# A fused attention, MLP and expert mixture: the last period of the MLP in another order, operand sums on VectorE, and loads of attention at other places

## The chip, the cores and the metric

One core of one Trainium2 chip runs the whole network in one launch. The metric is the device time of that core in microseconds, a median over runs.

## The reference

Three stages follow one another; each one's output is the next one's x.

```python
def _attn_ref(q, k, v, centroids):           # B=2, H=8, S=768, D=64, 16 clusters
    q_assign = np.argmax(np.einsum('bhsd,hcd->bhsc', q_n, c_n), axis=-1)   # likewise k_assign
    mask = q_assign[:, :, :, None] == k_assign[:, :, None, :]
    scores = np.where(mask, scale * np.matmul(q, k.transpose(0, 1, 3, 2)), -1000000000.0)
    attn = np.exp(scores - np.max(scores, axis=-1, keepdims=True))
    return np.matmul(attn / (attn.sum(-1, keepdims=True) + 1e-09), v)

def _moe_ref(x, w_gate, w_val, w_out):       # x 1536 x 512, d_ff 1536
    return (1.0 / (1.0 + np.exp(-(x @ w_gate)))) * (x @ w_val) @ w_out

def _moe2_ref(x, domain_probs, w1, w2):      # 4 experts, hidden 1024
    p = domain_probs / (domain_probs.sum(-1, keepdims=True) + 1e-09)
    for e in range(E):
        out += p[:, e:e + 1] * (np.maximum(x @ w1[e], 0.0) @ w2[e])
```

## The kernel before

**Numbers.** Every fp32 operand of a matmul is split into a high part, made by ScalarE, and a low part, the difference, made by VectorE or GpSimd. A product is three matmuls: high by high, high by low, low by high. Large products also go through seven block products in place of eight; for that, sums of operand blocks are formed first. In the profile a name that ends in h is a high part, in l a low part.

**Attention** takes eight pairs of heads with twelve items each, about 31 us to a pair. An item makes the scores of 128 queries, the exponentials, their transposes and, two items later, the product with V. The work of the next pair is hung beside the items by the table SLOT (line 35): an entry names an item, counted from the first one of the pair, and a place in it. `load_q` and `load_k` fetch Q and K as nq and nk. `q0` to `k1` transpose them and write the parts hiq, loq, hik, lok (lines 257 to 270). `rows0` and `rows1` (line 387) copy these parts by DMA to the operands L and R of the two heads, six DMAs for each. For each head the product with V leaves PSUM as U (line 472), which two DMAs carry to A and W. `spread` sends the row sums out to DRAM as rd and fetches them back, repeated over 64 partitions, as rb (lines 498 and 501); `xadd` and `xscale` then make the MLP's input. SyncE issues every DMA of the kernel, in program order, and waits there when one is not ready. The table SOON sets where the first raw weights of the MLP are loaded and converted.

**MLP.** `moe1` (line 847) runs six periods p over 256 hidden columns each, for two batches b of 768 tokens. TensorE's stages come in the order gate(p, 0), outp(p-1, 1), value(p, 0), gate(p, 1), outp(p, 0), value(p, 1). `gate` and `value` call `seven` (line 776): products 1, 6, 7, 5, 2, 4, 3 of six matmuls each with 384 columns, and between them VectorE combinations (lines 806 to 828) and pieces of side work, one list entry after each product. `outp` makes eight blocks, two halves n by four d, of six matmuls each, and adds each to acc. With `soon` it first sends the matmuls of the first outer block f = 0 to four banks of PSUM, and then those of f = 1. The raw weights are 64-bit words: a conversion is two ScalarE operations (658, 660), three on VectorE (665 to 667) and one on GpSimd (672). After it come four sums of blocks (702), the highs (710) and the lows w1l (711) of a unit in four groups, vs0 to vs3, where vs2 holds product 7 and vs3 product 4. An outer block has woh and wol (768, 769). `normalise` (167) scales the expert weights with four small VectorE operations.

**Mixture.** `operands` (1003) makes four operand sums (1019) from acc and the splits of seven operands Y (1015, 1016). `moe2` (1059) runs 32 pairs: `hidden` with `seven`, and `outp` with 36 matmuls of 512 columns.

Of the kernel before, what the change touches and what calls it, by code (L numbers as in the profile page):

```python
# [28 lines left out]
def r2(ap):  # L29
# [6 lines left out]
    "load_q": (-25, 0), "load_k": (-24, 2), "load_v": (-5, 2), "sq_q": (-19, 0), "sq_k": (-19, 0),  # L36
# [30 lines left out]
    "load01": (20, 2), "abs01": (25, 2), "bits01": (27, 36, 37), "low01": (27, 2), "round01": (38, 2),  # L67
    "load00": (32, 2), "abs00": (37, 2), "bits00": (39, 48, 49), "low00": (39, 2), "round00": (50, 2),
    "loado": (56, 2), "abso": (60, 2), "bitso": (61, 62, 63), "lowo": (61, 2), "roundo": (64, 2),
# [10 lines left out]
class Net:  # L80
# [85 lines left out]
    def normalise(self):  # L166
        nc, c = self.nc, self.cpool
        s = c.tile([128, B * NT], F32, name="pns")
        v = self.pn.rearrange("p b t e -> p (b t) e")
        nc.vector.tensor_reduce(s, v, axis=AX.X, op=ALU.add)  # L170
        nc.vector.tensor_scalar(s, s, 1e-9, None, op0=ALU.add)
        nc.vector.reciprocal(s, s)
        nc.vector.tensor_tensor(v, v, s.unsqueeze(2).to_broadcast([128, B * NT, E]), op=ALU.mult)
# [308 lines left out]
    def finish(self, n):  # L482
# [9 lines left out]
        def spread():  # L492
# [4 lines left out]
            d = self.dr.tile([2 * NT, 128], F32, name="rd", tag="rd", bufs=2)  # L497
            nc.sync.dma_start(out=d, in_=rT)
# [13 lines left out]
        return [("recip", recip), ("spread", spread), ("xadd", xadd), ("xscale", xscale)]  # L512
# [29 lines left out]
    def attention(self):  # L542
# [100 lines left out]
        spread, xadd, xscale = [go for at in sorted(work) for go in work[at]]  # L643
        spread()
        for _, g in pvs:
            list(g)
# [200 lines left out]
    def moe1(self, xadd, xscale):  # L847
# [35 lines left out]
        def outp(p, b, work=(), soon=False):  # L883
# [13 lines left out]
            def evict(ps, d, n):  # L897
                a = acc[:, d, b * S + n * HB:b * S + n * HB + HB]
                if p == 0:
                    nc.scalar.activation(a, ps, AF.Copy)  # L900
                else:
                    nc.vector.tensor_tensor(a, a, ps, op=ALU.add)  # L902
                if work:
                    for go in work.pop(0):
                        go()

            for n in range(2):
                c = slice(n * HB, n * HB + HB)
                if soon:
                    banks = [bank() for _ in range(4)]  # L910
                    for some in ((0, 1), (2,)) if n == 0 and (p == 0 or b == 1) else (range(3),):
# [25 lines left out]
        def total(u):  # L937
            return [lambda: u["sums"](Q)]
# [18 lines left out]
        value(0, 1, [load(U[1][1])] + [[go] for go in U[1][0]["split"]] + [[self.normalise]])  # L957
        for p in range(1, NP):
# [3 lines left out]
            if p + 1 < NP:  # L962
                g = U[p + 1][0]
                for go in load(g):
                    go()
            else:
                self.load_in2(0)
                self.load_in2(1)
            c = conv(o0)
            outp(p - 1, 1, [[vs[0]], [vs[1]], [vs[2]] + c[0], [vs[3]] + c[1], c[2], c[3], c[4]])  # L970
# [3 lines left out]
            if p + 1 < NP:  # L974
                c, d, split = conv(g, 0), conv(g, 1), g["split"]
                gate(p, 1, [e[0], e[1], e[2], e[3] + e[4], [o1["split"]] + c[0], c[1] + c[2], c[3] + c[4]])
                outers[2 * p + 2]["load"]()
                outp(p, 0, [d[0], d[1], d[2], d[3] + d[4], total(g), [split[0]], [], [split[1]]], soon=True)
                value(p, 1, [load(U[p + 1][1]), [split[2]], [split[3]]])
        gate(NP - 1, 1, [e[0], e[1], e[2], e[3] + e[4], [o1["split"]]])  # L980
        self.load_out2(0)
        out, cin = self.conv_out2(0), self.conv_in2(0)
        outp(NP - 1, 0, [[lambda: cin[0](Q)], [], [], [cin[1]], [cin[2]], [cin[3]], [cin[4]], []])
        Y = {o: (room(self.xp, "h%d" % o), room(self.xp, "l%d" % o)) for o in (0, 3, 4)}
        Y[5] = room(self.nat0, "nk"), room(self.nat0, "nq")
        Y[6] = room(self.xp, "tA"), room(self.xp, "tB")
# [4 lines left out]
        cin = self.conv_in2(1)  # L991
        value(NP - 1, 1, [[ys[0]], [lambda: ysplit(0, V), ys[1]], [ys[2]], [], [], [], [ys[3], lambda: ysplit(4, V)]])
        outp(NP - 1, 1, [[out[0], out[1], lambda: self.load_out2(1), lambda: ysplit(5, V), lambda: cin[0](Q)], [],
                         [lambda: ysplit(3, V)], [cin[1]], [lambda: ysplit(1, V)], [lambda: ysplit(6, Q)],
                         [cin[2]], [cin[3], cin[4]]], soon=True)
        self.last_split = lambda: ysplit(2, V)
# [9 lines left out]
    def operands(self, b, room):  # L1006
# [11 lines left out]
        add = nc.gpsimd if b == 0 else nc.vector  # L1018
        sums = [lambda o=o, x=x, z=z: add.tensor_tensor(o, x, z, op=ALU.subtract)
# [37 lines left out]
    def moe2(self):  # L1057
# [5 lines left out]
        def hidden(i, work):  # L1063
# [10 lines left out]
            if i == 0:  # L1074
                work = [[self.last_split]] + [[], []] + work
            self.seven(self.win2.pop(i)["w"], self.Y, [t[:, i % 2] for t in temps], split, [[], []][:2 - (i == 0)] + work[:2] + [[]] + work[2:])
# [38 lines left out]
        for i in range(LAST):  # L1115
            if i + 2 < LAST:
                self.load_in2(i + 2)
            hidden(i, (self.conv_out2(i + 1) if i + 1 < LAST else []) + late)
# [10 lines left out]
            else:  # L1129

                gap = [lambda: None] * (3 if i in (1, PER + 1) else 0)
# [91 lines left out]
```

## Time and profile before

| | |
|---|---|
| median of three runs | 1078.47 us (1076.16 to 1079.19) |
| the profiled execution | 1079.04 us, its span 1077.0 us |
| TensorE matmul busy (PE) | 1037.7 us, 96% |
| VectorE / ScalarE / GpSimd busy (DVE, ACT, POOL) | 822.0 / 547.3 / 640.0 us |
| mean granted clock of TensorE | 0.992 |

Attention lies at about 31 to 284 us of the span, the MLP at 284 to 573, the mixture behind it. PE means matmuls, PEld weight loads, SP SyncE. A row of waits names the waiting engine and line, what ended the wait, then the total, the number of times and the longest. A row of windows gives for a stretch its length, and the busy time and instructions of each engine, then the granted clock, the share of the DMA engines and their rate. A row of the timeline gives the start, the duration (the sum, where rows are merged) and the instruction; in brackets is the engine's idle time before it and what ended that. A row of groups ends with busy time, mean ns of one, and idle time.

### The profile page before, as it was taken

The page shows a single profiled execution, that of the slowest core. Times are in us where ns is not written, and L with a number is a line of the kernel's source. Part 1 is how long each engine was busy: PE and PEld are TensorE (multiplying, and loading weights), DVE is VectorE, ACT ScalarE, POOL GpSimd, SP SyncE. Part 2 cuts the span into 40 slices and gives each one's busy share as a digit, 9 for nine tenths or more (in the row PEclk, how much of TensorE's full clock was granted, in tenths as well). Part 3 has the DMA queues.
Part 4 walks back from the last instruction along what each step waited for, and adds up shares of the span by engine and source line. Part 5 has one row for each costly group of instructions (what it writes and reads, how often), then busy time and mean ns, then how long its engine had stood idle before and what let it go on. Part 6 is the DMA issues. An engine that isn't in the chain of part 4 may idle for free. (4 is left out here: it accounts for less than half of the span.)

```text
span 1077.0 us, 16228 instructions
## 1 busy us (share of the span) xinstructions
PE 1037.7 (96%) x5813; PEld 962.8 (89%) x5813; DVE 822.0 (76%) x1404; ACT 547.3 (51%) x1155; POOL 640.0 (59%) x572
## 2 busy tenths in 40 slices
PE   6999989899989999999998999999999999999998
PEld 5899989898889999999997889989998999899887
DVE  6998989799886776877765877677668867776765
ACT  4888989789665444444443433333334433333320
POOL 7566777767876677676786644444445644444430
PEclk8999999999999999999999999999999999999999
DMA  8678767654212222212111222122122312221201
GB/s 177 139 165 189 180 150 174 139 134 135 65 40 60 60 78 79 64 54 79 59 40 59 79 79 61 58 79 79 50 69 99 118 41 77 79 78 40 79 20 59
DMA packets 86480, 95.86 MB, mean 89 GB/s; under 512 B 42720, under 2 KB 59456, under 8 KB 86400
## 3 DMA queue, kind: packets, MB, share of 16 engines
q1 hardware_dynamic: 86256, 94.80, 32.7%
q8 instruction: 46, 0.75, 0.3%
q14 instruction: 34, 0.28, 0.1%
q10 hardware_dynamic: 144, 0.03, 0.0%
HBM read 65.07 MB, written 3.19 MB: 63 GB/s over the span
## 5 line engine op out<-in xcount | busy, mean ns | idle before, releaser
L1051 POOL TENSOR_TENSOR wol<-r,woh 128x512 fp32r<-128x512 f32 x62 | 80.0, 1292 | 157.6 <-ACT woh L1050 157.4
L1103 DVE SCALAR_TENSOR_TENSOR acc<-po,pn,acc 128x512 f32<-128x512 f32 (+1 forms) x181 | 129.8, 743 | 36.3 <-PE po L1098 36.3
L1098 PE MATMUL po<-woh,h2l 128*128 128x512 f32 (+1 forms) x374 | 145.7, 389 | 0.0
L1097 PE MATMUL po<-wol,h2h 128*128 128x512 f32 (+1 forms) x374 | 145.6, 389 | 0.0
L1096 PE MATMUL po<-woh,h2h 128*128 128x512 f32 (+1 forms) x374 | 145.0, 388 | 0.0
L711 POOL TENSOR_TENSOR w1l<-sf,w1h 128x512 fp32r<-128x512 f32 x88 | 114.0, 1317 | 42.7 <-ACT w1h L710 42.7
L1070 ACT ACTIVATE h2h<-ph 128x384 fp32r<-128x384 f32 x128 | 62.6, 490 | 119.2 <-PE ph L793 87.6
L793 PE MATMUL ph<-h,w1h 128*128 128x384 f32 x336 | 113.6, 338 | 2.3 <-DVE sg L877 1.5
L793 PE MATMUL ph<-h,w1l 128*128 128x384 f32 x336 | 112.8, 336 | 0.0
L793 PE MATMUL ph<-l,w1h 128*128 128x384 f32 x336 | 112.5, 335 | 0.0
L456 DVE TENSOR_TENSOR pl<-T,ph 128x384 fp32r<-128x384 f32 x192 | 97.6, 549 | 18.3 <-ACT ph L455 16.6
L892 PE MATMUL po<-G,woh 128*128 128x384 f32 x384 | 104.3, 340 | 3.9 <-DVE acc L902 2.0
L710 ACT ACTIVATE w1h<-sf 128x512 fp32r<-128x512 f32 x88 | 55.7, 633 | 91.6 <-DVE sf L702 68.0
L1071 DVE SCALAR_TENSOR_TENSOR h2l<-ph,h2h 128x384 fp32r<-128x384 f32 x128 | 71.0, 554 | 36.5 <-ACT h2h L1070 33.4
L432 PE MATMUL S<-R,L 80*128 80x384 f32 (+1 forms) x384 | 92.2, 363 | 0.8 <-ACT P L443 0.7
L435 DVE TENSOR_REDUCE nm<-S 128x1 f32<-128x768 f32 x96 | 91.1, 949 | 2.0 <-PE S L432 1.4
L455 ACT ACTIVATE ph<-T 128x384 fp32r<-128x384 f32 x192 | 84.4, 493 | 14.5 <-PE T L452 13.9
L711 POOL TENSOR_TENSOR w1l<-r,w1h 128x512 fp32r<-128x512 f32 x64 | 67.7, 1059 | 36.7 <-ACT w1h L710 36.7
L443 ACT ACTIVATE P<-S,nm 128x768 f32<-128x768 f32 x96 | 87.7, 914 | 2.1 <-DVE nm L435 2.1
L452 PE MATMUL T<-ident,P 128*128 128x128 f32 x576 | 82.5, 278 | 1.8 <-DVE pl L456 1.5
L1098 PEld LDWEIGHTS po<-woh,h2l 128*128 128x128 f32 x374 | 70.2, 188 | 14.5
L1096 PEld LDWEIGHTS po<-woh,h2h 128*128 128x128 f32 x374 | 70.2, 188 | 13.9
(275 smaller groups left out, 2781.3 us busy)
## 6 DMA issues: line engine op xcount, KB each, us to landing
r<-in_moe_w_dram SPq DMA_DIRECT2D x64, 512.0 KB, 3.8
L<-hiq SPq DMA_DIRECT2D x32, 192.0 KB, 4.7
R<-hik SPq DMA_DIRECT2D x32, 192.0 KB, 4.6
raw<-in_moe_w_val_dram SPq DMA_DIRECT2D x12, 512.0 KB, 3.7
rwo<-in_moe_w_out_dram SPq DMA_DIRECT2D x11, 512.0 KB, 3.5
raw<-in_moe_w_gate_dram SPq DMA_DIRECT2D x10, 512.0 KB, 3.8
nq<-in_q_dram SPq DMA_DIRECT2D x16, 192.0 KB, 5.4
nk<-in_k_dram SPq DMA_DIRECT2D x16, 192.0 KB, 4.4
```

The lines of the kernel that those rows point to most:

```text
L432: nc.tensor.matmul(ps[:, a, 0:384], l[0:k, c], r[0:k, a * 384:a * 384 + 384], start=l is L1, stop=l is L2)
L435: nc.vector.tensor_reduce(nm, ps[:, :, 0:384], axis=AX.XY, op=ALU.max, negate=True)
L443: nc.scalar.activation(r2(pt), ps[:, :, 0:384], AF.Exp, bias=nm, scale=1.0, accum_out=P["sums"][:, i:i + 1])
L455: nc.scalar.activation(hi, ps, AF.Copy)
L456: nc.vector.tensor_tensor(lo, ps, hi.bitcast(F32), op=ALU.subtract)
L711: nc.gpsimd.tensor_tensor(lo[:, sl], x, hi[:, sl].bitcast(F32), op=ALU.subtract)
L793: nc.tensor.matmul(ps, x[:, a, j], y[:, j], start=first and j == 0 and k == 0, stop=j == 1 and k == 2, skip_group_check=not first)
L892: nc.tensor.matmul(ps, t[x][:, dc], y[:, f, c], start=f == 0 and k == 0, stop=f == 1 and k == 2)
L1096: nc.tensor.matmul(ps, Hh[:, f, c], wh[:, dc], start=f == 0, stop=False)
L1097: nc.tensor.matmul(ps, Hh[:, f, c], wl[:, dc], start=False, stop=False)
L1098: nc.tensor.matmul(ps, Hl[:, f, c], wh[:, dc], start=False, stop=f == 1)
L1103: nc.vector.scalar_tensor_tensor(a, ps, pe, a, op0=ALU.mult, op1=ALU.add)
```

## The change

In attention K is loaded four items earlier, Q about one; the raw weight loads of SOON move by one item; rb is fetched in a step of its own, two items after rd. In the MLP `soon` acts on the first half alone; outp(0, 1) leaves PSUM on VectorE; `normalise` is spread over that stage; and the last period takes the order gate(5, 0), outp(4, 1), value(5, 0), outp(5, 0), gate(5, 1), value(5, 1), outp(5, 1). There the outer block 11 gets tiles of its own (raw, and "of" in cv), and outer 10 and 11 are both converted in outp(4, 1). The operand sums of batch 0 are made on VectorE. Weights of the mixture's first pairs are converted at other places.

```diff
-    "load_q": (-25, 0), "load_k": (-24, 2), "load_v": (-5, 2), "sq_q": (-19, 0), "sq_k": (-19, 0),
+    "load_q": (-26, 2), "load_k": (-28, 2), "load_v": (-5, 2), "sq_q": (-19, 0), "sq_k": (-19, 0),
...
-    "mask0": (-5, 1), "mask1": (-4, 2), "v0": (-2, 0), "v1": (-1, 0), "recip": (10, 0), "spread": (12, 1),
+    "mask0": (-5, 1), "mask1": (-4, 2), "v0": (-2, 0), "v1": (-1, 0), "recip": (10, 0), "spread": (12, 1), "rb": (14, 0),
...
-    "load01": (20, 2), "abs01": (25, 2), "bits01": (27, 36, 37), "low01": (27, 2), "round01": (38, 2),
+    "load01": (21, 2), "abs01": (25, 2), "bits01": (27, 36, 37), "low01": (27, 2), "round01": (38, 2),
...
-        nc.vector.tensor_reduce(s, v, axis=AX.X, op=ALU.add)
-        nc.vector.tensor_scalar(s, s, 1e-9, None, op0=ALU.add)
-        nc.vector.reciprocal(s, s)
-        nc.vector.tensor_tensor(v, v, s.unsqueeze(2).to_broadcast([128, B * NT, E]), op=ALU.mult)
+        return [lambda: nc.vector.tensor_reduce(s, v, axis=AX.X, op=ALU.add),
+                lambda: nc.vector.tensor_scalar(s, s, 1e-9, None, op0=ALU.add),
+                lambda: nc.vector.reciprocal(s, s),
+                lambda: nc.vector.tensor_tensor(v, v, s.unsqueeze(2).to_broadcast([128, B * NT, E]), op=ALU.mult)]
...
-            d = self.dr.tile([2 * NT, 128], F32, name="rd", tag="rd", bufs=2)
-            nc.sync.dma_start(out=d, in_=rT)
+            P["rd"] = self.dr.tile([2 * NT, 128], F32, name="rd", tag="rd", bufs=2)
+            nc.sync.dma_start(out=P["rd"], in_=rT)
+
+        def repeat():
+            d = P["rd"]
             rb = P["rb"] = self.xsp.tile([128, NT, 128], F32, name="rb", tag="rb", bufs=1)
...
-        return [("recip", recip), ("spread", spread), ("xadd", xadd), ("xscale", xscale)]
+        return [("recip", recip), ("spread", spread), ("rb", repeat), ("xadd", xadd), ("xscale", xscale)]
...
-        spread, xadd, xscale = [go for at in sorted(work) for go in work[at]]
+        spread, repeat, xadd, xscale = [go for at in sorted(work) for go in work[at]]
         spread()
+        repeat()
         for _, g in pvs:
...
-                if p == 0:
+                if p == 0 and b == 0:
                     nc.scalar.activation(a, ps, AF.Copy)
+                elif p == 0:
+                    nc.vector.tensor_copy(a, ps)
                 else:
...
-                if soon:
+                if soon and n == 0:
                     banks = [bank() for _ in range(4)]
-                    for some in ((0, 1), (2,)) if n == 0 and (p == 0 or b == 1) else (range(3),):
+                    for some in ((0, 1), (2,)) if p in (0, NP - 1) else (range(3),):
                         for d in range(4):
...
-        value(0, 1, [load(U[1][1])] + [[go] for go in U[1][0]["split"]] + [[self.normalise]])
+        value(0, 1, [load(U[1][1])] + [[go] for go in U[1][0]["split"]])
         for p in range(1, NP):
             v, (o0, o1) = U[p][1], outers[2 * p:2 * p + 2]
             c, d, vs = conv(v, 0), conv(v, 1), v["split"]
             gate(p, 0, [c[0], c[1] + d[0], c[2], c[3] + c[4], d[1] + d[2], d[3] + d[4], total(v)])
-            if p + 1 < NP:
-                g = U[p + 1][0]
-                for go in load(g):
-                    go()
-            else:
-                self.load_in2(0)
-                self.load_in2(1)
+            if p + 1 == NP:
+                break
+            g = U[p + 1][0]
+            for go in load(g):
+                go()
             c = conv(o0)
-            outp(p - 1, 1, [[vs[0]], [vs[1]], [vs[2]] + c[0], [vs[3]] + c[1], c[2], c[3], c[4]])
+            n = self.normalise() if p == 1 else [lambda: None] * 4
+            outp(p - 1, 1, [[vs[0], n[0]], [vs[1], n[1]], [vs[2], n[2]] + c[0], [vs[3], n[3]] + c[1], c[2], c[3], c[4]])
             o1["load"]()
             value(p, 0, [[], [o0["split"]]])
             e = conv(o1)
-            if p + 1 < NP:
-                c, d, split = conv(g, 0), conv(g, 1), g["split"]
-                gate(p, 1, [e[0], e[1], e[2], e[3] + e[4], [o1["split"]] + c[0], c[1] + c[2], c[3] + c[4]])
-                outers[2 * p + 2]["load"]()
-                outp(p, 0, [d[0], d[1], d[2], d[3] + d[4], total(g), [split[0]], [], [split[1]]], soon=True)
-                value(p, 1, [load(U[p + 1][1]), [split[2]], [split[3]]])
-        gate(NP - 1, 1, [e[0], e[1], e[2], e[3] + e[4], [o1["split"]]])
+            c, d, split = conv(g, 0), conv(g, 1), g["split"]
+            gate(p, 1, [e[0], e[1], e[2], e[3] + e[4], [o1["split"]] + c[0], c[1] + c[2], c[3] + c[4]])
+            outers[2 * p + 2]["load"]()
+            outp(p, 0, [d[0], d[1], d[2], d[3] + d[4], total(g), [split[0]], [], [split[1]]], soon=True)
+            value(p, 1, [load(U[p + 1][1]), [split[2]], [split[3]]])
+        f = 2 * NP - 1
+        o1 = outers[f] = self.outer(f, self.raw.tile([128, 2, 256], I64, name="raw", tag="raw"),
+                                    self.cv.tile([128, 2, 512], F32, name="of", tag="cv")[:, 0])
+        o1["load"]()
+        self.load_in2(0)
+        c, e = conv(o0), conv(o1)
+        outp(NP - 2, 1, [[vs[0]], [vs[1]] + c[0], c[1], c[2], c[3] + c[4], [vs[2]] + e[0], e[1] + e[2], e[3] + e[4]])
         self.load_out2(0)
+        self.load_in2(1)
+        value(NP - 1, 0, [[o0["split"]], [vs[3]], [o1["split"]]])
         out, cin = self.conv_out2(0), self.conv_in2(0)
-        outp(NP - 1, 0, [[lambda: cin[0](Q)], [], [], [cin[1]], [cin[2]], [cin[3]], [cin[4]], []])
+        outp(NP - 1, 0, [[lambda: cin[0](Q)], [], [out[0]], [], [out[1]]], soon=True)
+        self.load_out2(1)
         Y = {o: (room(self.xp, "h%d" % o), room(self.xp, "l%d" % o)) for o in (0, 3, 4)}
         Y[5] = room(self.nat0, "nk"), room(self.nat0, "nq")
-        Y[6] = room(self.xp, "tA"), room(self.xp, "tB")
         t = self.xp.tile([128, 4, 2, HB], F32R, name="Y0", tag="R0")
         Y[1], Y[2] = (t[:, 0], t[:, 1]), (t[:, 2], t[:, 3])
         self.Y = Y
         ys, ysplit = self.operands(0, [room(self.opx, t, F32) for t in ("h1", "l1", "h2", "l2")])
-        cin = self.conv_in2(1)
-        value(NP - 1, 1, [[ys[0]], [lambda: ysplit(0, V), ys[1]], [ys[2]], [], [], [], [ys[3], lambda: ysplit(4, V)]])
-        outp(NP - 1, 1, [[out[0], out[1], lambda: self.load_out2(1), lambda: ysplit(5, V), lambda: cin[0](Q)], [],
-                         [lambda: ysplit(3, V)], [cin[1]], [lambda: ysplit(1, V)], [lambda: ysplit(6, Q)],
-                         [cin[2]], [cin[3], cin[4]]], soon=True)
-        self.last_split = lambda: ysplit(2, V)
+        gate(NP - 1, 1, [[ys[0]], [ys[1]], [ys[2]], [lambda: ysplit(0)], [lambda: ysplit(4)]])
+        Y[6] = room(self.xp, "tA"), room(self.xp, "tB")
+        value(NP - 1, 1, [[cin[1]], [cin[2], lambda: ysplit(5)], [ys[3]], [], [], [], [lambda: ysplit(3)]])
+        self.late2 = late = self.conv_in2(1)
+        outp(NP - 1, 1, [[cin[3]], [lambda: ysplit(1)], [cin[4]], [lambda: late[0](Q)], [lambda: ysplit(6)], [],
+                         [late[1]]], soon=True)
+        self.last_split = lambda: ysplit(2)
...
-        add = nc.gpsimd if b == 0 else nc.vector
-        sums = [lambda o=o, x=x, z=z: add.tensor_tensor(o, x, z, op=ALU.subtract)
+        sums = [lambda o=o, x=x, z=z: nc.vector.tensor_tensor(o, x, z, op=ALU.subtract)
...
-        def hidden(i, work):
+        def hidden(i, work, sides=None):
...
-            if i == 0:
-                work = [[self.last_split]] + [[], []] + work
-            self.seven(self.win2.pop(i)["w"], self.Y, [t[:, i % 2] for t in temps], split, [[], []][:2 - (i == 0)] + work[:2] + [[]] + work[2:])
+            self.seven(self.win2.pop(i)["w"], self.Y, [t[:, i % 2] for t in temps], split,
+                       sides or [[], []] + work[:2] + [[]] + work[2:])
...
-            hidden(i, (self.conv_out2(i + 1) if i + 1 < LAST else []) + late)
+            out = self.conv_out2(i + 1) if i + 1 < LAST else []
+            sides = None
+            if i == 0:
+                c = self.late2
+                sides = [[c[2]], [self.last_split], [c[3]], [], [c[4]], out]
+            elif i == 1:
+                sides = [[lambda c=late[0]: c(nc.gpsimd)], [late[1]], [], [], [late[2]], [late[3]], [late[4]]]
+            hidden(i, out + late, sides)
...
-                gap = [lambda: None] * (3 if i in (1, PER + 1) else 0)
+                gap = out + [lambda: None] if i == 1 else [lambda: None] * (3 if i == PER + 1 else 0)
```

In SyncE's order, at the second pair of heads, a pair's loads, row copies and returns stand as follows. Before, from the raw weight load to the next head's first row copies:

```order
L724 DMA R_61<-in_moe_w_gate_dram 128x2x256
L479 DMA A<-U 64x768
L480 DMA W<-U 64x768
L179 DMA nq<-in_q_dram 128x6x64 x2
...
L498 DMA rd<-rTs 12x128
L501 DMA rb<-rd 64x768 x2
L179 DMA nk<-in_k_dram 128x6x64 x2
L479 DMA A<-U 64x768
L480 DMA W<-U 64x768
L395 DMA R_1531<-hik 64x768 x2
```

Now:

```order
L179 DMA nk<-in_k_dram 128x6x64 x2
L479 DMA A<-U 64x768
L480 DMA W<-U 64x768
L728 DMA R_61<-in_moe_w_gate_dram 128x2x256
L179 DMA nq<-in_q_dram 128x6x64 x2
...
L498 DMA rd<-rTs 12x128
L504 DMA rb<-rd 64x768 x2
L479 DMA A<-U 64x768
L480 DMA W<-U 64x768
L395 DMA R_1531<-hik 64x768 x2
```

K's two DMAs moved from behind rb to ahead of A and W of the first head; rd and rb still stand one behind the other.

On GpSimd, from outp(4, 1) into value(5, 0). Before:

```order
L711 TENSOR_TENSOR w1l<-cv,w1h 128x512
L711 TENSOR_TENSOR w1l<-sf,w1h 128x512 x2
L711 TENSOR_TENSOR w1l<-cv,w1h 128x256
L672 TENSOR_TENSOR co<-co,rwo 128x512
L769 TENSOR_TENSOR wol<-co,woh 128x512
```

Now:

```order
L715 TENSOR_TENSOR w1l<-cv,w1h 128x512
L715 TENSOR_TENSOR w1l<-sf,w1h 128x512
L676 TENSOR_TENSOR co<-co,rwo 128x512
L715 TENSOR_TENSOR w1l<-sf,w1h 128x512
L676 TENSOR_TENSOR of<-of,raw 128x512
L773 TENSOR_TENSOR wol<-co,woh 128x512
L715 TENSOR_TENSOR w1l<-cv,w1h 128x256
L773 TENSOR_TENSOR wol<-of,woh 128x512
```

Both conversions of outer blocks now end ahead of lows that value(5, 0) reads: co's ahead of vs2's, of's and wol ahead of vs3's (the 256 wide one).

On VectorE in gate(5, 1), ph, u and m being the stage's own tiles. Before:

```order
L806 TENSOR_TENSOR u_6711<-m_6710,ph_6724 128x384
L665 TENSOR_SCALAR co<-co 128x512
L810 TENSOR_TENSOR u_6712<-u_6711,ph_6733 128x384
L666 TENSOR_SCALAR co<-co 128x512
L814 TENSOR_TENSOR ph_6733<-u_6712,ph_6742 128x384
L667 SCALAR_TENSOR_TENSOR co<-rwo,co 128x512
L823 TENSOR_TENSOR ph_6764<-u_6712,ph_6764 128x384
```

Now:

```order
L908 TENSOR_TENSOR acc_4118<-acc_4118,po 128x384 x8
L1031 TENSOR_TENSOR h_6808<-acc_4118 128x768
L810 TENSOR_TENSOR u_6814<-m_6813,ph_6825 128x384
L1031 TENSOR_TENSOR l_6809<-acc_4118,h_6808 128x768
L814 TENSOR_TENSOR u_6815<-u_6814,ph_6834 128x384
L1031 TENSOR_TENSOR h_6810<-l_6809,acc_4118 128x768
L818 TENSOR_TENSOR ph_6834<-u_6815,ph_6843 128x384
L1029 TENSOR_TENSOR l_6800<-acc_4118,h_6799 128x768
L1029 TENSOR_TENSOR l_6804<-l_6809,h_6803 128x768
L827 TENSOR_TENSOR ph_6863<-u_6815,ph_6863 128x384
```

Three operand sums (h_6808, l_6809, h_6810) and two splits took the place of one conversion, and the splits stand ahead of line 827, which was line 823.

## Rows read from the trace of the kernel before

**Rows 1.** TensorE's waits over the span: total us, times, longest.

```profile
PE PV L465 <- ACT U L472: 7.1, 6, 2.6
...
PE po L1096 <- DVE acc L1101: 2.1, 1, 2.1
PE ph L793 <- DVE Y L1016: 2.0, 1, 2.0
...
PE T L257 <- DMA nk<-in_k_dram: 1.7, 1, 1.7
...
PE ph L793 <- DVE sg L877: 1.5, 1, 1.5
```

**Rows 2.** Windows of one pair of heads in attention.

```profile
80.00:93.00 13.00, 13.00 (x91) 12.74 (x90) 12.14 (x22) 12.60 (x33) 12.53 (x12) 1.00 1.00 222
93.00:96.00 3.00, 3.00 (x25) 2.96 (x24) 2.94 (x7) 2.86 (x7) 1.23 (x1) 1.00 0.04 14
96.00:106.00 10.00, 8.60 (x59) 8.08 (x58) 8.06 (x15) 6.97 (x18) 2.59 (x2) 1.00 1.05 232
```

**Rows 3.** Timeline of ScalarE and of SyncE's issues at the same pair.

```profile
104.38 0.49 ACT L266 ACTIVATE hik<-T 128x384 fp32r<-128x384 f32 x1 [1.61 <-DMA R<-hik]
...
94.65 1.11 SPq L501 DMA_DIRECT2D rb<-rd  x2
```

**Rows 4.** Windows behind three waits, for the granted clock.

```profile
139.00:142.50 3.50, 3.50 (x15) 3.50 (x14) 2.66 (x5) 2.83 (x7) 3.19 (x3) 0.51 0.15 28
203.85:207.30 3.45, 3.45 (x17) 3.28 (x18) 2.38 (x4) 3.17 (x7) 3.44 (x3) 0.51 0.08 14
575.90:579.30 3.40, 3.07 (x10) 3.07 (x11) 3.40 (x6) 0.49 (x1) 3.40 (x3) 0.50 0.00 0
```

**Rows 5.** Windows of outp(1, 1), of two second halves under soon, and of outp(0, 0).

```profile
376.00:384.32 8.32, 8.32 (x49) 8.32 (x49) 5.11 (x9) 4.30 (x8) 6.81 (x8) 1.00 0.43 126
...
355.72:361.09 5.37, 4.95 (x25) 4.21 (x25) 4.54 (x10) 1.28 (x3) 3.01 (x3) 1.00 0.36 98
...
498.72:504.06 5.34, 4.92 (x25) 4.19 (x25) 4.53 (x10) 1.27 (x3) 2.98 (x3) 1.00 0.32 98
...
292.12:301.29 9.17, 8.92 (x48) 8.37 (x49) 7.71 (x6) 6.92 (x13) 8.52 (x6) 1.00 0.01 2
```

**Rows 6.** Window of outp(0, 1), and both ways of leaving PSUM, by line.

```profile
327.02:336.64 9.62, 8.62 (x50) 8.30 (x49) 4.34 (x6) 6.73 (x15) 7.98 (x9) 1.00 0.40 110
...
L900 ACT ACTIVATE acc<-po x16: 468/488/502, 295.3 to 336.8; 128x384 f32<-128x384 f32 x16
...
L902 DVE TENSOR_TENSOR acc<-acc,po x80: 539/548/555, 355.2 to 577.0; 128x384 f32<-128x384 f32 x80
```

**Rows 7.** Windows of the MLP's last period, and of outp(5, 0) in it.

```profile
511.34:600.01 88.67, 81.42 (x433) 76.36 (x433) 61.25 (x100) 37.77 (x72) 67.19 (x58) 0.98 0.17 54
542.20:551.89 9.69, 8.79 (x49) 8.29 (x49) 4.44 (x8) 3.40 (x7) 8.98 (x10) 1.00 0.20 54
```

**Rows 8.** TensorE's waits in 572 to 582 us.

```profile
PE ph L793 <- DVE ph L814: 0.8, 1, 0.8
```

**Rows 9.** Groups by line and shape in 340 to 540 us: a conversion's steps.

```profile
L665 DVE TENSOR_SCALAR co<-co 128x512 f32<-128x512 f32 x9 | 10.4, 1153 | 8.6 <-POOL w1l L711 8.6
...
L667 DVE SCALAR_TENSOR_TENSOR co<-rwo,co 128x512 int32<-128x512 int32 x9 | 6.4, 715 | 0.0
...
L672 POOL TENSOR_TENSOR co<-co,rwo 128x512 int32<-128x512 int32 x9 | 11.8, 1307 | 12.7 <-DVE co L667 12.7
L769 POOL TENSOR_TENSOR wol<-co,woh 128x512 fp32r<-128x512 f32 x9 | 11.6, 1292 | 6.7 <-ACT woh L768 6.7
...
L711 POOL TENSOR_TENSOR w1l<-cv,w1h 128x256 fp32r<-128x256 f32 x8 | 6.6, 830 | 0.0
```

**Rows 10.** Operand sums and splits by line: minimum, median and maximum in ns.

```profile
L1019 DVE TENSOR_TENSOR acc<-acc x4: 949/950/950, 616.4 to 662.9; 128x768 f32<-128x768 f32 x4
...
L1016 DVE TENSOR_TENSOR l<-acc,h x3: 949/1300/2255, 554.7 to 812.9; 128x768 fp32r<-128x768 f32 x3
```

More of the change, by code (lines that the diff above doesn't have):

```diff
@@ L66 @@
 SOON = {
-    "load01": (20, 2), "abs01": (25, 2), "bits01": (27, 36, 37), "low01": (27, 2), "round01": (38, 2),
-    "load00": (32, 2), "abs00": (37, 2), "bits00": (39, 48, 49), "low00": (39, 2), "round00": (50, 2),
-    "loado": (56, 2), "abso": (60, 2), "bitso": (61, 62, 63), "lowo": (61, 2), "roundo": (64, 2),
+    "load01": (21, 2), "abs01": (25, 2), "bits01": (27, 36, 37), "low01": (27, 2), "round01": (38, 2),
+    "load00": (33, 2), "abs00": (37, 2), "bits00": (39, 48, 49), "low00": (39, 2), "round00": (50, 2),
+    "loado": (57, 2), "abso": (60, 2), "bitso": (61, 62, 63), "lowo": (61, 2), "roundo": (64, 2),
 }
```

## The prediction

> **What bounds the kernel.** The table of engines comes first: TensorE is busy 1037.7 of 1077.0 us, so apart from a slower clock no more than about 39 us can go. The list of TensorE's waits says where they lie. The reader should see there that no wait is long: 7.1 us in six pieces behind U, 1.7 behind K's load, 2.0 and 2.1 where the MLP ends, 1.5 behind sg [rows 1]. The windows then price a stage: outp takes 8.32 us undisturbed [rows 5], and whatever is above that is disturbance. Last, the windows behind three waits show a second price: the granted clock reads 0.51, 0.51 and 0.50 [rows 4]. That is the lower of the two levels (1.2 GHz against 2.4), and in some 3.4 us it costs half, **1.7 us**.
>
> The sum is made against the profiled execution, 1079.04 us, which lies 0.6 above the median shown.
>
> **Attention.** ScalarE works in order. At line 266 it waits 1.61 us until the row copies have left hik; U's eviction stands behind it, and TensorE behind that [rows 3]. So the end of the copies R<-hik counts. DMA is full in two bursts per pair, at shares of 1.00 and 1.05, and between them lie 3 us at 0.04 [rows 2], the return of the sums, after which rb is issued at 94.65 [rows 3]. K's 384 KB leave the second burst and join the first; at 222 GB/s [rows 2] that is 1.77 us. The own step for rb moves nothing, since rd and rb remain neighbours in SyncE's order, and rb is still queued behind rd's landing. The raw weights go behind A and W, within the same burst. If rd is delayed by as much as the first burst grows, the copies land when they did. If it is not, they land up to 1.77 us earlier and nearly all of the 7.1 us could go. I take a fifth to a quarter, 1.4, because rb's issue follows the end of the first burst by under 2 us, nearer to the first case. K's own wait of 1.7 [rows 1] goes, as K is issued some 10 us earlier, and with it half of one clock drop, 0.8. Together **-3.9**, bounds 0 and -12.3 (7.1 + 1.7 + two drops). Next late there is the same thing again, R<-hik.
>
> What would speak against even this is in the Trainium skill, "DMA: Bandwidth & Descriptors", section "Issuing engines are not separate DMA queues": all DMAs run on the same 16 engines and interleave. By it a transfer that is only moved frees no bandwidth, and the term would be near zero in place of -3.9. The traffic on both sides of the gap agrees with it, the gap itself doesn't.
>
> **Soon in the first half only.** In periods 1 to 4 the second half of outp(p, 0) takes 5.37 to 5.34 us (first and last of four) where half of 8.32 is 4.16 [rows 5]: 1.2 each, 4.8 in all. TensorE there needs all four banks before any block is finished, while VectorE empties them at 0.548 us each [rows 6]. In the plain order it needs one bank per block of 1.04 us (8.32 / 8), nearly twice that time, so this excess is covered; if VectorE is late with other work, up to a tenth of a us each comes back. outp(0, 0) takes 9.17, 0.85 above [rows 5], and I give its second half 0.5. Less 0.3 for remnants: **-5.0**, bounds -4 and -5.6.
>
> **Normalise and outp(0, 1).** Four small VectorE operations delay the last combination, and TensorE waits 1.5 behind sg [rows 1]. Spread over eight evictions they have room: -1.4. outp(0, 1) takes 9.62, 1.3 above 8.32 [rows 6]; ScalarE's evictions there stand in a queue with highs and conversions. On VectorE one takes 0.548 against 0.488 us [rows 6], eight of them 0.5 us more, but VectorE has time in a block of 1.04. I take -1.2: together **-2.6**, bounds -1.5 and -2.8.
>
> The Trainium skill, "VectorE: DVE Perf Modes", in the section on the TRN2 errata, gives (120 + 384)/0.96, so 525 ns, for VectorE from PSUM and (172 + 384)/1.2, so 463, for ScalarE. The durations agree in sense, and by durations alone the move would lose 0.5 us in place of gaining 1.2. The window with its 1.0 us of idle speaks for the queue ahead as what counts, so I don't follow it.
>
> **The last period, what goes.** Its 88.67 us hold 81.42 busy [rows 7], 7.25 idle, and one clock drop of 1.7. outp(5, 0) has 9.69 - 8.79 = 0.9 idle [rows 7]: product and wol come too late, since outer 11 is converted just ahead; now it is converted two stages earlier. In front of the mixture stand 2.0 behind Y [rows 1] and 0.8 behind ph [rows 8], because the last splits are queued among acc evictions. Now they stand in gate(5, 1) to outp(5, 1). The 2.1 behind acc [rows 1] goes as VectorE takes its evictions ahead of the sums sf. With the clock drop: 0.9 + 2.8 + 2.1 + 1.7 = **-7.5**; the rest of the idle time stays.
>
> **The last period, what comes.** In value(5, 0): outer 11's conversion ends on VectorE at the end of outp(4, 1), eight evictions (4.4) and six steps beside them. By the groups a first step is 1.15 and a last one 0.72 [rows 9]; with the middle one like the last, six come to 5.2, so 9.6 us of work in a stage of 8.32, which starts 1 to 1.5 late with the last combinations: of is ready 2 to 2.6 us after value(5, 0) began. GpSimd then rounds it (1.31), makes wol (1.29) and only then vs3's low (0.83) [rows 9], at 5.5 to 6.0 or later. Product 4, five products in, wants it at 5 x 1.04 = 5.2; vs2's low, behind co, is short by some tenths at product 7. I take **+2.7**, bounds 1 and 4.5.
>
> In gate(5, 1) and value(5, 1): VectorE makes three sums and two splits between its combinations. One such operation takes 0.95 us alone and a median of 1.30, at most 2.26, in the stretches where GpSimd also works [rows 10]. Both splits wait for ScalarE's highs and stand ahead of line 827, which finishes product 4. So that ends some 2 us late, at about 9.2 us in a stage of 7.28; value's product 6 wants the bank of product 4 at 8.3 and waits 1.2 to 1.9, product 3 of value(5, 1) another 1 to 2 behind ys3 and the split of operand 5, product 1 some 0.6. I take **+4.2**, bounds 1.5 and 5.5. In both places such a wait could drop the clock; I take half a drop, **+0.9**, bounds 0 and 3.4. Outer loads and the mixture's loads are issued early and I cost them at nothing: DMA is at 0.17 in the period [rows 7]; without that cover each would cost its landing, a few us. The three matmuls of hidden(0)'s first product that now stand ahead of outp(5, 1) cost nothing, as they are work that was due anyway. Net for the period: -7.5 + 7.8 = **+0.3**, bounds -7.5 (nothing comes) and +5.9.
>
> **Sum.** -3.9 - 5.0 - 2.6 + 0.3 = -11.2: 1067.8, and less the 0.6 to the median **1067** (rounded).
>
> **The rivals.**
> - *Bytes are conserved and the last period only exchanges waits for waits.* Attention gives 0: 1067 + 4 = **1071**. With the last period's waits at +3 it is 1074. This is also the case in which part of the change does nothing, as with rb's step. For: shares of 1.00 and 1.05 on both sides of the gap. Against: K's own wait was there to take. Chance 0.20.
> - *The new waits don't come.* Conversions and sums fit between the evictions, the period yields 7.5 in place of losing 0.3: 1067 - 7.8 = **1059**; with attention's waits all gone as well, 1051. For: GpSimd loses the four slow sums. Against: the fixed order in front of line 827. Chance 0.15.
> - *Slower.* A longer first burst delays rows and rd by 1.77, the second is no shorter in effect, and at five pairs the wait behind hik becomes long enough to drop the clock each time: 5 x (1.77 + 1.7) = 17.4 in place of -3.9, so 1067 + 21.3 = **1088**. It decides from the point where attention loses more than 10.5, as 7.3 are gained elsewhere and 3.2 more are needed. For: two drops follow such waits already [rows 4]. Against: the bytes ahead of R<-hik remain equal. Chance 0.05.
> - *No difference*, if attention loses 4 to 11 or the new waits reach 8 to 15 us: about 1077. Chance 0.05.
>
> **How the numbers follow.** The forecast has 0.55. 0.3% of 1078 is 3.2 us, about what a measurement of this kernel tells from no change. Faster takes the forecast and the first two rivals, 0.90; the others 0.05 each. The forecast's own bounds, taken at half their width since they will hardly all meet, give 1060 to 1073. The range reaches into the first rival, to 1075, and into the second, to 1056; beyond lie some 0.05 below and 0.13 above.
>
> **What would show it.** Right: second halves of outp(1, 0) to (4, 0) at 4.2, no wait behind sg at normalise, outp(0, 1) near 8.4; no wait behind K's load; GpSimd's w1l (256 wide) ending after 5.2 us of value(5, 0); a wait of TensorE on sg or ph at the start of value(5, 1). Wrong: waits of the same sum behind U with K moved would kill the attention term; value(5, 0) and gate(5, 1) at their 7.3 us would say that the chain of conversions fits; waits behind K or U above 10 us in sum would be the slower case.

## The result, and the profile after

The changed kernel took 1063.70 us (median of four, 1062.61 to 1068.87) against 1078.76 for the kernel before: a ratio of 0.9875, with a 95% interval from 0.9839 to 0.9910. Run again on another occasion it took 1066.02 (six runs), ratio 0.9897 [0.9873, 0.9920]. The forecast was 1067, the range 1056 to 1075.

The profiled execution is the slowest of the first four, 1068.87 us. A second profile of the changed kernel was 2.4 us shorter, all of it in attention. This table, from the starts of the stages in each trace, shows it (us):

| stretch | before | after | after, again |
|---|---|---|---|
| start to gate(0, 0) | 272.5 | 272.2 | 269.9 |
| gate(0, 0) to value(1, 0) | 64.15 | 61.70 | 61.75 |
| value(1, 0) to gate(5, 0) | 174.71 | 171.85 | 171.73 |
| gate(5, 0) to the second outp of the mixture | 95.97 | 91.64 | 91.67 |
| the rest | 469.71 | 469.70 | 469.68 |

So outside attention the change gave 2.4 + 2.9 + 4.3 = **9.6 us**, the same in both profiles.

TensorE's waits over the span of the changed kernel, which answer to [rows 1]:

```profile
PE PV L465 <- ACT U L472: 7.1, 6, 3.3
...
PE ph L797 <- ACT sg L869: 2.9, 4, 1.4
...
PE ph L797 <- POOL w1l L715: 2.4, 2, 1.3
...
PE ph L797 <- DVE sg L881: 0.3, 2, 0.2
```

K's load, Y and the mixture's acc are gone from the list, and sg behind VectorE is down from 1.5 to 0.3; new are 2.4 behind w1l and more behind ScalarE's sg. Behind U it is 7.1 again. Windows of the changed kernel, which answer to [rows 5], [rows 6] and [rows 7]: two second halves of outp(p, 0), outp(0, 0), outp(0, 1), value(1, 0), the last period, and in it value(5, 0), outp(5, 0), gate(5, 1) and value(5, 1). The last period's window here reaches to the second outp of the mixture, as in the table (95.97 before); that of [rows 7] ends 7.3 us sooner, at the end of the first.

```profile
353.82:358.27 4.45, 4.43 (x25) 4.27 (x25) 4.45 (x10) 0.72 (x2) 2.17 (x2) 1.00 0.39 118
...
494.05:498.45 4.40, 4.40 (x25) 4.29 (x25) 4.40 (x10) 0.67 (x2) 2.12 (x2) 1.00 0.40 119
291.83:300.46 8.63, 8.63 (x48) 8.38 (x49) 7.18 (x6) 7.12 (x14) 8.54 (x6) 1.00 0.01 2
325.57:333.89 8.32, 8.32 (x50) 8.32 (x49) 5.74 (x13) 4.18 (x8) 6.67 (x8) 1.00 0.45 127
333.89:341.89 8.00, 7.84 (x43) 7.02 (x42) 7.34 (x13) 2.07 (x6) 5.81 (x5) 1.00 0.20 64
505.73:597.37 91.64, 86.87 (x475) 82.22 (x475) 67.92 (x112) 41.51 (x81) 67.90 (x63) 1.00 0.18 58
521.68:531.91 10.23, 7.84 (x44) 7.20 (x43) 8.09 (x13) 3.06 (x6) 8.07 (x8) 1.00 0.32 104
531.91:540.83 8.92, 8.66 (x49) 8.23 (x49) 5.26 (x10) 2.03 (x4) 8.28 (x10) 1.00 0.00 0
540.83:548.16 7.33, 7.33 (x43) 7.13 (x42) 5.05 (x8) 2.15 (x5) 0.31 (x1) 1.00 0.19 72
548.16:558.16 10.00, 8.02 (x44) 7.18 (x43) 7.58 (x12) 4.38 (x9) 3.32 (x2) 1.00 0.01 2
```

value(5, 0) and value(5, 1) are 3.0 and 2.7 us above 7.28, as forecast in kind, yet the clock stays at 1.00 throughout the period. In gate(5, 1) GpSimd has 0.31 us of work. The timeline of GpSimd from outp(4, 1) into value(5, 0):

```profile
523.84 1.45 POOL L715 TENSOR_TENSOR w1l<-sf,w1h 128x512 fp32r<-128x512 f32 x1
526.77 1.31 POOL L676 TENSOR_TENSOR of<-of,raw 128x512 int32<-128x512 int32 x1 [1.48 <-PE ph L797]
528.04 1.28 POOL L773 TENSOR_TENSOR wol<-co,woh 128x512 fp32r<-128x512 f32 x1
529.28 0.72 POOL L715 TENSOR_TENSOR w1l<-cv,w1h 128x256 fp32r<-128x256 f32 x1
```

The last low, for product 4, ends at 530.0, that is 8.3 us into value(5, 0), behind of and wol. GpSimd's idle time ahead of "of" is a wait for VectorE, whose part of outer 11's conversion ends only 5.0 us into the stage:

```profile
525.96 0.68 DVE L671 SCALAR_TENSOR_TENSOR of<-raw,of 128x512 int32<-128x512 int32 x1
```

On VectorE in gate(5, 1):

```profile
547.76 0.96 DVE L1029 TENSOR_TENSOR l<-acc,h 128x768 fp32r<-128x768 f32 x1 [1.35 <-ACT h L1028]
548.88 0.96 DVE L1029 TENSOR_TENSOR l<-l,h 128x768 fp32r<-128x768 f32 x1 [0.16 <-ACT h L1028]
549.75 0.56 DVE L827 TENSOR_TENSOR ph<-u,ph 128x384 f32<-128x384 f32 x1
```

Product 4's combination (line 827) waits for both splits, as the order had said, and ends 9.5 us after gate(5, 1) began.

### The profile page after: what moved, and what is told of

Read it like the earlier page. It is cut to its first block, busy times and chain, and to the rows that moved or that the text cites. A ratio compares the mean times of both kernels' runs of the same rounds, so it can differ in the third digit from the quotient of the medians.

```text
span 1067.1 us, 16230 instructions
## 1 busy us (share of the span) xinstructions
PE 1035.5 (97%) x5813; PEld 961.9 (90%) x5813; DVE 825.2 (77%) x1413; ACT 545.0 (51%) x1147; POOL 635.3 (60%) x571
## 4 chain that ended last, share of the span: by engine, by line
PE 64%; DVE 4%; issue 2%; POOL 2%; ACT 1%; DVEq 0%; ACTq 0%; POOLq 0%
PE ph L797 32%; PE po L1108 8%; PE po L1109 8%; PE po L1107 8%; PE po L896 7%; DVE ph L832 1%; DVE sg L881 1%; POOL G L883 0%; POOL sf L706 0%; DVE ph L827 0%; DVE ph L818 0%; ACT sg L869 0%; DVE u L814 0%; DVE h2l L1083 0%; POOL cv L676 0%
## 5 line engine op out<-in xcount | busy, mean ns | idle before, releaser
L896 PE MATMUL po<-G,woh 128*128 128x384 f32 x384 | 101.1, 337 | 0.6 <-ACT G L882 0.3
```

The lines of the kernel that those rows point to most:

```text
L896: nc.tensor.matmul(ps, t[x][:, dc], y[:, f, c], start=f == 0 and k == 0, stop=f == 1 and k == 2)
```

## The experiments

Ten further kernels ran, and the changed one again. This table has their times, the stretches of each profile in the order of the table above, and the runs' medians; "the change" is the kernel after.

| kernel | median (runs), us | ratio to before [95%] | start | 0 | 1 to 4 | last |
|---|---|---|---|---|---|---|
| again | 1066.02 (6) | 0.9897 [0.9873, 0.9920] | 269.9 | 61.75 | 171.73 | 91.67 |
| no_att | 1063.84 (4) | 0.9872 [0.9845, 0.9899] | 266.6 | 61.72 | 171.76 | 91.63 |
| att_old | 1066.83 (6) | 0.9910 [0.9882, 0.9937] | 268.8 | 61.68 | 171.78 | 91.63 |
| last_only | 1069.66 (4) | 0.9924 [0.9900, 0.9948] | 268.4 | 64.13 | 174.59 | 91.78 |
| no_soon | 1069.13 (6) | 0.9922 [0.9897, 0.9948] | 265.4 | 61.69 | 175.55 | 91.75 |
| rb_late | 1063.62 (6) | 0.9867 [0.9846, 0.9889] | 267.1 | 61.73 | 171.73 | 91.64 |
| pool_sums | 1064.13 (4) | 0.9880 [0.9852, 0.9908] | 267.2 | 61.69 | 171.72 | 90.52 |
| last_fix | 1065.68 (4) | 0.9886 [0.9857, 0.9916] | 272.7 | 61.70 | 171.62 | 90.35 |
| no_norm | 1068.13 (1) | | 270.8 | 62.89 | 171.36 | 91.58 |
| no_acc | 1063.50 (1) | | 266.0 | 63.43 | 170.91 | 91.62 |
| best | 1062.07 (4) | 0.9856 [0.9825, 0.9888] | 268.4 | 61.73 | 171.70 | 89.92 |

Stretches outside attention repeat within a quarter of a us where nothing in them was changed. The total scatters over several us from one execution to the next, so small differences are read from the stretches.

**The change again** (no edit).

> The changed kernel once more, with a second profile. The first profiled execution took 1068.87 us, the other three 1062.6 to 1063.7. Theory: attention's waits behind U and the row copies vary between executions, and the profiled one had a bad one (a single wait of 3.3 us and a clock drop behind it); then a second profile comes at 1063 to 1064 and its sum of waits behind U is under 4 us. Rival: the profile itself costs this kernel 5 us; then it is at 1068 to 1069 again with the waits behind U at 7 us.

Neither quite: the second profiled execution was 2.4 us shorter, all of it in attention, with a wait of 2.7 us left at the same place and 5.3 in sum behind U. The runs reach from 1063.99 to 1070.76, and the profiled one, 1066.48, lies among them: the profile costs nothing that shows.

**Attention's tables back, first try** (no_att).

```diff
-    "load_q": (-26, 2), "load_k": (-28, 2),
+    "load_q": (-25, 0), "load_k": (-24, 2),
...
-    "load01": (21, 2),
+    "load01": (20, 2),
...
-    "load00": (33, 2),
+    "load00": (32, 2),
...
-    "loado": (57, 2),
+    "loado": (56, 2),
```

> The change without its attention part (K, Q and the raw weight loads at their old items). Theory from the two traces, in which attention ends 0.3 us earlier: moving K moves bytes only, so 1064 us (within 1 of the changed kernel). Rival: the 5 us by which the timed runs beat the profiled one are the attention part's, then 1068 to 1069. My forecast's term of 3.9 would give 1067.6.

1063.84 fits the theory in number, but not for its reason. With K at its old item, rb's own step takes effect: SyncE issues K while rd is under way. Its issues in this kernel:

```profile
89.04 0.85 SPq L498 DMA_DIRECT2D rd<-rTs  x1
89.94 1.70 SPq L179 DMA_DIRECT2D nk<-in_k_dram  x2
95.26 1.78 SPq L504 DMA_DIRECT2D rb<-rd  x2
```

The DMA share in the gap of [rows 2] is there 1.08 in place of 0.04. In the change it is 0.67, but there the gap only moved, to 95 to 98 us, where it is 0.09. First no_att, then the change:

```profile
93.00:96.00 3.00, 3.00 (x25) 2.96 (x25) 2.89 (x7) 2.85 (x8) 0.00 (x0) 1.00 1.08 162
```

```profile
95.00:98.00 3.00, 3.00 (x24) 2.90 (x23) 2.97 (x8) 2.61 (x6) 0.22 (x1) 1.00 0.09 31
```

So this was another version of the attention part and not its absence.

**The last period alone** (last_only: soon, normalise, the evictions of outp(0, 1) and attention's tables as before, with rb's step kept).

> The kernel before with the new last period alone (order, conversions, sums on VectorE, evictions of the first mixture pair). Theory from the traces (95.98 us before, 91.64 now, from gate(5, 0) to the second outp of the mixture): 4.3 less than before, 1074.4. My forecast's term (+0.3) would give 1079. Rival: part of it hangs on the other edits, then 1076 to 1078.

The period shows the 4.2 us of the theory (95.97 to 91.78), with everything else in the MLP as before. The kernel gained 8.9. The remainder, 4.7, is attention's, where again rb's step took effect with K at its old place. This part of the expectation missed it.

**Attention really as before** (att_old: as no_att, and rb next to rd).

```diff
-"rb": (14, 0),
+"rb": (12, 1),
```

> The change without its attention part, now really: K, Q and the raw weights at their old items and rb right behind rd, so that SyncE's order in attention is that of the kernel before (in no_att rb's step took effect, since K stood between rd and rb). Theory: the rest is worth 2.4 + 2.9 + 4.3 = 9.6 us, so 1069; attention's part of the change is then worth the difference to 1064 to 1066, and rb behind K alone (no_att) as much or more. Rival: attention's order makes no difference beyond its scatter between executions, then 1064 to 1066.

1066.83 (1064.40 to 1070.48) lies between both. Less the 9.6 the kernel before would be at 1068.5 to 1069; this is 2 less with the same order in attention. The change's own attention order gave 1065.5 as the median over all ten runs (1062.61 to 1070.76), 1.3 less than att_old and 3 less than the kernel before less 9.6. The gain of attention is between these, and the scatter doesn't let it be told more closely.

**Rb behind the row copies** (rb_late: as no_att).

```diff
-"rb": (14, 0),
+"rb": (16, 2),
```

> As no_att, but rb two items later still, behind the row copies of the first head: nothing of 384 KB and no round trip stands ahead of R<-hik any more. Theory: these copies are what attention waits for; they land some 4 us earlier, the waits behind U at three places (1.2, 1.1, 1.7 in no_att) fall under 0.5 each, 2 to 4 us less than no_att: 1060 to 1062. Rival: rb's user xscale comes late on GpSimd or the waits only change their name: 1063 to 1066.

1063.62, level with no_att: the rival's number. Yet the waits went as the theory said: at the pair of [rows 3] ScalarE's hik no longer waits, and the list of TensorE's and ScalarE's waits in 60 to 250 us has

```profile
PE PV L465 <- ACT U L472: 0.5, 2, 0.3
...
ACT hik L266 <- DMA R<-hik: 0.4, 1, 0.4
```

where no_att has 4.3 and 4.6, the change 5.6 and 6.8. That execution lost time at another place instead: TensorE waits 1.3 us behind VectorE's oh at 198.4 us, with a clock drop behind it, and in best 2.5 us at the same place. In rb_late's trace VectorE waits there, ahead of oh, 2.1 us for GpSimd's w (line 318), which stands behind operand sums of the MLP (line 529); no run moves these.

**Soon in both halves** (no_soon).

```diff
-                if soon and n == 0:
+                if soon and (n == 0 or p < NP - 1):
...
-                    for some in ((0, 1), (2,)) if p in (0, NP - 1) else (range(3),):
+                    for some in ((0, 1), (2,)) if n == 0 and p in (0, NP - 1) else (range(3),):
```

> The change with soon in both halves again in periods 0 to 4. Theory: outp(p, 0) goes from 8.6 back to 9.5 us four times (3.7) and outp(0, 0) from 8.6 to 9.2 (0.5): 4.2 more than the changed kernel, near 1068. My forecast's 5.0 would give 1068.7. Rival: the time comes back in the stages behind it, then under 2 more.

Periods 1 to 4 went up by 3.7 us (175.55 against 171.85), the theory's figure; the runs by 3.1 to 5.4. The half us of outp(0, 0) did not count: that stage took 9.19 in place of 8.63, and gate(0, 1) behind it 8.54 in place of 9.12, so its stretch stayed at 61.69.

**Normalise in one place** and **outp(0, 1) on ScalarE** (no_norm, no_acc).

```diff
-        value(0, 1, [load(U[1][1])] + [[go] for go in U[1][0]["split"]])
+        value(0, 1, [load(U[1][1])] + [[go] for go in U[1][0]["split"]] + [self.normalise()])
...
-            n = self.normalise() if p == 1 else [lambda: None] * 4
+            n = [lambda: None] * 4
```

```diff
-                if p == 0 and b == 0:
+                if p == 0:
                     nc.scalar.activation(a, ps, AF.Copy)
-                elif p == 0:
-                    nc.vector.tensor_copy(a, ps)
```

> The change with the four operations of normalise together again at the end of value(0, 1). Theory: they delay the last combination there by 1.9 us; TensorE waits 1.4 to 1.5 behind sg, and the stretch from gate(0, 0) to value(1, 0) goes from 61.7 to 63.1. Rival: the stages behind it, which take 0.7 more in the change than before (value(1, 0)), give it back: under 62.4.

> The change with outp(0, 1) leaving PSUM on ScalarE again. Theory: ScalarE's queue of highs and conversions stands ahead of the evictions, outp(0, 1) takes 9.6 in place of 8.3 us, and the stretch from gate(0, 0) to value(1, 0) goes from 61.7 to 62.5 to 63. Rival: by the durations alone ScalarE is the faster one (0.49 against 0.55 us), then 61.2 to 61.7.

No_norm has the wait back (1.5 behind sg), its stretch is 1.2 longer and the next 0.5 shorter: 0.7 net. No_acc has a wait of 1.2 behind ScalarE's acc, 1.7 more in its stretch and 0.9 less in the next: 0.8 net. TensorE's waits in 300 to 345 us, of no_norm and of no_acc:

```profile
PE ph L797 <- DVE sg L881: 1.5, 1, 1.5
...
PE po L896 <- ACT acc L904: 1.2, 1, 1.2
```

No_acc's rival (61.2 to 61.7) failed; its stretch, 63.43, is even above the theory. No_norm's 62.89 lies between its theory and its rival. In both value(1, 0), which takes 8.00 us in the change, 7.56 in no_norm and 7.28 in no_acc, gives part of the loss back.

**The sums on GpSimd** (pool_sums).

```diff
-        sums = [lambda o=o, x=x, z=z: nc.vector.tensor_tensor(o, x, z, op=ALU.subtract)
+        add = nc.gpsimd if b == 0 else nc.vector
+        sums = [lambda o=o, x=x, z=z: add.tensor_tensor(o, x, z, op=ALU.subtract)
```

> The change with the four operand sums of batch 0 on GpSimd. Theory: in gate(5, 1) GpSimd was idle for 11 us and the sums took 0.95 each on VectorE beside no other work, so neither engine is short there; the last period stays at 91.6 us within 0.6. Rival (the sums belong on VectorE): on GpSimd they take 1.8 each, the splits come later, and the period is 1.5 to 3 us longer.

The period is 1.1 us shorter, outside the theory's bounds and against the rival. One sum takes 1.83 to 1.85 us on GpSimd and 0.95 on VectorE, but on GpSimd the trace has nobody waiting for it:

```profile
L1032 POOL TENSOR_TENSOR h<-acc x1: 1833/1833/1833, 536.0 to 536.0; 128x768 f32<-128x768 f32 x1
```

Value(5, 1) takes 8.49 us in place of 10.00: its waits behind sg and line 818 fall from 1.4 and 0.6 to 0.9 and nothing. The stretch from outp(5, 1) on takes 0.4 longer. With the new order, the sums on VectorE are a small loss.

**Two orders altered in the last period** (last_fix).

```diff
-outp(NP - 2, 1, [[vs[0]], [vs[1]] + c[0], c[1], c[2], c[3] + c[4], [vs[2]] + e[0], e[1] + e[2], e[3] + e[4]])
+outp(NP - 2, 1, [[vs[0]], [vs[1]], [vs[2]] + c[0], [vs[3]] + c[1], c[2], c[3] + c[4] + e[0], e[1] + e[2], e[3] + e[4]])
...
-        value(NP - 1, 0, [[o0["split"]], [vs[3]], [o1["split"]]])
+        value(NP - 1, 0, [[o0["split"]], [], [o1["split"]]])
...
-[lambda: ysplit(0)], [lambda: ysplit(4)]])
+[lambda: ysplit(0, Q)], [lambda: ysplit(4, Q)]])
```

> The change with two orders altered in the last period: vs2 and vs3 stand ahead of the conversion of outer 11, and the two splits of gate(5, 1) make their lows on GpSimd. Theory: value(5, 0) loses its two waits behind w1l (1.1 and 1.3) and goes from 10.2 to under 8.2 us; the wait behind sg at value(5, 1) (1.4) goes, so that stage falls from 10.0 to under 9; the last period from 91.6 to 88 to 88.5. Rival: outer 11 is then late for outp(5, 0), and the lows on GpSimd for the matmuls that read them, and the period stays at 91 to 92.

The period fell by 1.3 to 90.35, not by 3 to 4. The waits behind w1l and sg are gone from the list, but TensorE then waits for VectorE at two places: 1.0 in value(5, 0) behind line 810, ahead of which of's conversion stands, and 1.3 in value(5, 1) behind line 818, ahead of which ys3 stands. In outp(5, 0) it waits for GpSimd's G. Its waits in 503 to 595 us:

```profile
PE ph L797 <- DVE ph L818: 1.3, 1, 1.3
PE ph L797 <- DVE u L810: 1.0, 1, 1.0
PE po L896 <- POOL G L883: 0.7, 1, 0.7
```

**All of it together** (best: rb_late's tables, sums on GpSimd, the splits of gate(5, 1) at its end, outer 11 converted in value(5, 0) with wol on VectorE).

```diff
-outp(NP - 2, 1, [[vs[0]], [vs[1]] + c[0], c[1], c[2], c[3] + c[4], [vs[2]] + e[0], e[1] + e[2], e[3] + e[4]])
+outp(NP - 2, 1, [[vs[0]], [vs[1]], [vs[2]] + c[0], [vs[3]] + c[1], c[2], c[3], c[4], e[0]])
...
-        value(NP - 1, 0, [[o0["split"]], [vs[3]], [o1["split"]]])
+        value(NP - 1, 0, [[o0["split"]] + e[1], e[2], e[3] + e[4], [], [lambda: o1["split"](V)]])
...
-[lambda: ysplit(0)], [lambda: ysplit(4)]])
+[], [], [lambda: ysplit(0)], [lambda: ysplit(4)]])
```

> The change with what the runs point to: attention's order of rb_late, the four sums on GpSimd, the two splits of gate(5, 1) behind the last combinations, and outer 11 converted in value(5, 0) with its low on VectorE. Theory: the last period falls by 1.1 (sums) + 0.9 (wait behind sg) + 1.5 to 2.5 (waits behind w1l) from 91.6 to 87 to 88.2 us, so 3.5 to 4.5 us less than rb_late: 1059 to 1060. Rival: the waits of value(5, 0) move into outp(5, 0), where the low of outer 11 comes late; then the period takes 89 to 90.5 and the kernel 1061 to 1063.

1062.07 us, ratio 0.9856 [0.9825, 0.9888]: its interval overlaps that of the change. The rival's numbers came: the period takes 89.92. Outp(5, 0) takes 10.31 in place of 8.92, but TensorE waits there for the lows and highs of G, not for the low of outer 11: of the 1.4 behind GpSimd's G, 0.9 lies in outp(5, 0) and 0.5 in outp(5, 1).

## Why the prediction was right, and where its steps were not

The sum came out near the result partly by luck, as its errors had opposite signs: the last period gave 4.6 us more than forecast, soon 1.3 less, normalise with outp(0, 1) 1.1 less, and attention about 1 less by the runs.

- **Attention, -3.9.** Two profiles show -0.3 and -2.6, the runs some 3. K's own wait went, as said, and a whole clock drop with it: from the pair's first P on ScalarE to that of the next pair, the pair that held both took 35.00 us before and 31.95 after. In the first profile two other pairs grew by 0.7 and 1.5; the waits behind U, from which 1.4 was to go, sum to 7.1 and 5.3 in the two profiles (7.1 before). That K's bytes only move was right: in the profile after, rb is issued at 96.51 in place of 94.65 [rows 3], by 1.86 us later, where K's 384 KB were costed at 1.77, the gap moved with it, and hik's wait stays (1.23 for 1.61). The Trainium skill, "DMA: Bandwidth & Descriptors", section "Issuing engines are not separate DMA queues", has all DMAs interleave on the same 16 engines; the later rb fits that. That rb's step moves nothing was also right, but the step didn't see why: K's move takes the load away that would stand between rd and rb. At its old place K fills the gap (no_att).
- **Soon, -5.0.** Shown by no_soon at -3.7 for the four periods; the second halves take 4.40 to 4.45 and not 4.16. VectorE is busy without a break in them (4.45 of 4.45 us), and where "up to a tenth of a us each" was costed for its other work, 0.24 to 0.29 came. The half us of outp(0, 0) came (9.17 to 8.63 [rows 5]) and was given back in gate(0, 1) at once, as no_soon shows.
- **Normalise and outp(0, 1), -2.6.** Both waits went, 1.2 in gate(1, 0) and 1.3 in outp(0, 1), but value(1, 0) takes 0.7 more; undone one at a time they are worth 0.7 and 0.8. The steps that failed are "they have room" and "VectorE has time in a block of 1.04": the next outer block's conversion and the last evictions run on, to 338.6, into value(1, 0), whose window above has 0.16 idle and 0.7 too much. The Trainium skill, "VectorE: DVE Perf Modes", in the section on the TRN2 errata, has VectorE as the slower engine for this eviction; an estimate from its figures (525 against 463 ns, eight times) would make no_acc 0.5 faster. The traces agree on the durations (0.546 against 0.492 us in the change), but no_acc was 0.8 slower net.
- **The last period, +0.3: what goes.** The period failed most: -4.3 was measured. What goes was costed at 7.5; from outp(5, 1) to the mixture's second outp the traces show 48.15 us before and 39.21 after, 8.9 less where the step had 6.6. Of these 2.3, waits of 1.2 are the small idle pieces that I had left standing between the interleaved matmuls, behind A (0.5), acc (0.4) and G (0.3); they went too. The rest is in no listed wait.
- **The last period: what comes.** This was costed at 7.8. Value(5, 0) took 2.95 more (2.7 forecast), but that size is partly luck: the order was as described, yet VectorE's part of outer 11's conversion ended 5.0 us into the stage (2 to 2.6 forecast), product 4's low at 8.3 (5.5 to 6.0), and the wait fell in two parts, 1.1 at product 7 (some tenths forecast) and 1.3 at product 4. Gate(5, 1) and value(5, 1) took 2.7 more (4.2 forecast): product 6 waited 1.4 as forecast, product 3 only 0.6 (1 to 2) and product 1 not at all (0.6). The sums had been costed beside GpSimd's work, at 1.30 to 2.26 us [rows 10]; GpSimd was idle in gate(5, 1), and three of the four took 0.951, the last 1.59. The clock drop cost 0 (0.9 forecast).

Of the rivals, the first was right on bytes and wrong on the period. The second failed, as the new waits came. The slower one did not come: TensorE's wait behind U grew at one pair (3.3 for 2.6) and not at five.

Three readings of the prediction need a correction that leaves the forecast as it is. "No difference" wants new waits of 8 to 15 us on top of the 7.8 already in the sum. The bounds at half width give 1059 and not 1060 below. And the list of waits has two long ones that the text passes over, 5.0 behind oh and 2.9 behind identb, both before 20 us of the span; they are 4.3 and 2.9 after.

## What to carry to other kernels

Before an operation is moved between two engines, look at whether the other one is idle in that very stretch: here GpSimd at half the speed was better than VectorE, because nothing waited behind it (pool_sums, 1.1 us). A round trip to DRAM in an in-order DMA queue costs what could have been issued in its wait; put a load that is due anyway between its two halves, and check that another part of the same change doesn't take that load away. And price a removed disorder by its whole stretch, from the last clean stage to the next, not by its listed waits.

## What was not expected of the hardware

The two profiles of the changed kernel differ in attention alone, and its runs by up to 8 us. In attention DMA is full in bursts, waits of 1 to 3 us come or not, and behind some of them the granted clock falls to 0.5 for 3.4 us, in best for 6.8. The length of the wait alone doesn't tell whether a drop follows: in pool_sums one of 1.88 us that ended at 106.0 had none behind it, in rb_late one of 1.28 us that ended at 198.4 had.
